# Cached attention with a token mixer: the first keys turned inside the query projection, and a head's closing matmuls placed right behind scores

## The chip, the core and the metric

The kernel runs on one core of a Trainium2 chip. The core has five engines that run in parallel, each with its own queue of instructions that it works off in order: TensorE (PE in the profile), VectorE (DVE), ScalarE (ACT), GpSimd (POOL) and SyncE (SP), which here only issues transfers. They wait for each other through semaphores. Sixteen DMA engines move data between the chip's large memory (HBM) and the core's own (SBUF); matmuls write to a third memory, PSUM, of eight banks. The metric is the time of one execution in microseconds; less is better.

## The reference

Eight sequences, one token each, of width 512. The normalized token is projected to 32 query heads of 128; each group of four query heads shares one of 8 cached key/value heads of 8192 positions. The attention's output is projected back to 512. Beside it runs a mixer whose token axis has length 1, so that it is a sum over 1792 hidden units of a gelu at every one of the 8 x 512 elements. Everything is float32.

```python
xn = layernorm(x)                                # (8, 1, 512)
q = (xn @ wq) as (b, 32 heads, 1, 128)
p = softmax(q . k_cache * 128**-0.5)             # k_cache, v_cache: (8, 8, 8192, 128)
a = (p . v_cache) as (b, 1, 4096) @ wo           # four query heads per cached head
u = gelu(layernorm(xn)[b, d] * w1[f] + b1[f])    # (b, 512, 1792)
return x + a + sum_f u * w2[f] + b2
```

Keys and values are 64 pieces of 4 MB each; all else that is read is small beside them, but for the two projection matrices of 8 MB.

## The kernel before

The work is cut into 64 *pairs* (a cached head h and a sequence b), eight pairs to a head, in the order h, b. One pair takes 4 MB of keys and 4 MB of values. Two buffers hold keys (K, tiles k0 and k1) and two hold values (V, v0 and v1), picked by whether b is even. At the start the value buffers hold the query projection's matrix (`load_wq`, L59). In what follows "key n" and "value n" are those of pair n, counted from the program's start or within a head.

A pair is `slot` (L336). Its instructions are written in one order for all engines, and each engine keeps that order:

- `q_place` (L211) spreads the next pair's query into a weight tile W.
- `qk` (L222) computes the scores of this pair into a PSUM tile (S), 16 matmuls of 512 columns. They need the key *turned*, that is transposed in blocks on VectorE.
- `load(K, ...)` (L65) issues the key after next. Its buffer is the one that `qk` has just read, so it waits for these scores.
- `turn` (L218) transposes the next pair's key, a quarter at a time; the four calls are strewn over the slot. They wait for that key to land.
- `sm_max`, `sm_bias`, `sm_exp`, `sm_place` (L231 to L246) are the softmax: a maximum on VectorE, a small matmul (L236) and two VectorE steps for the bias, the exponential on ScalarE, a matmul (L245) and a transpose on VectorE that put the probabilities in place (PT).
- `pv` (L250) multiplies the pair before's probabilities with its values; `load(V, ...)` behind it issues the next pair's value into the buffer of the pair before, so it waits for these matmuls.
- `o_pick` and `o_place` (L257, L263) gather the result of the pair before into the PSUM tile MH.

Once per head there is more. In the head's first pair (b = 0) stand `o_sums` (L273: the softmax denominators of the last head, four matmuls and a reciprocal) ahead of the exponential, and behind `sm_place` come `o_scale`, `o_project` (L283: the output projection of the last head) and `mx_begin` (L293: a matmul that spreads the mixer's input for this head, and its copy to SBUF by ScalarE). The mixer itself has 14 steps per head (`mx_step`, L300), a gelu on ScalarE and a multiply and an add on GpSimd each, two behind each pair from b = 0 on (three behind each pair in the last head, b = 1 to 4). `mx_end` (L306) sums GpSimd's accumulator ACC into the output with four small matmuls, at the end of a head's last pair (of pair 5 in the last head). `load_wo` (L75) fetches the 1 MB of projection weights for the head, behind pair 2.

The first pair is written ahead of a loop, the loop's body holds pairs 1 to 7 of a head and pair 0 of the next, and the last head's pairs are written out behind it (L382 to L415), with a tail of its own for pairs 6 and 7. Inside the loop the instructions wait by counts within a stage of two pairs; a wait of the loop's first instructions on work ahead of the loop is a wait for the last such work of that engine.

The profile's names: `s` scores, `o` value products, `mh` the tile MH, `misc` the three small PSUM tiles, `pr` and `pt` probabilities before and after placing, `mr`, `sq`, `nb` the softmax's maximum and bias, `macc` the mixer's accumulator, `g` a gelu, `hb` the mixer's input, `om` and `ob` the gathered values.

## Time and profile before

| | us |
|---|---|
| median of 3 runs | 1311.59 (1311.26 to 1312.59) |
| the profiled execution | 1310.17 |
| its span, first to last instruction | 1306.7 |
| DVE busy | 814.9 (62%) |
| PE busy | 788.5 (60%) |
| ACT busy | 289.4 (22%) |
| POOL busy | 252.3 (19%) |
| DMA engines busy, mean over the span | 99% |
| mean granted TensorE clock | 0.764 of full |

The span is what the trace shows; the execution's time has some 3.5 us around it. In the rows below, a view of groups or of a timeline has the start in us, the duration in us, the engine, the line of the kernel, the operation and the tiles (out <- in); a chain has start, duration and what it was. `SPq` is the issue of a transfer, not the transfer itself.

### The profile page before, as it was taken

To read this page: it belongs to the slowest core of one execution; us is meant where nothing else is said; L and a number is where in the kernel's file an instruction comes from. 1 tells how busy PE (TensorE), PEld (TensorE's weight loads), DVE (VectorE), ACT (ScalarE), POOL (GpSimd) and SP (SyncE) were. 2 spreads that over 40 slices of the span, in tenths; PEclk is the share of its full clock that TensorE was granted. 3 is DMA by queue.
4 is the path that set the end of the run, shared out by engine and by line. 5 is a ranking of instruction groups with operands and counts; after the bars stand their busy time and mean duration, and the time that the engine had idled before them with its cause. 6 is when DMAs were issued, how large, how long until landed. Compare 5 with 4: busy or idle time off the path is not lost.

```text
span 1306.7 us, 13701 instructions
## 1 busy us (share of the span) xinstructions
PE 788.5 (60%) x5178; PEld 257.3 (20%) x5178; DVE 814.9 (62%) x860; ACT 289.4 (22%) x365; POOL 252.3 (19%) x226
## 2 busy tenths in 40 slices
PE   3466465755477475665566664575655864757657
PEld 2111112211122121211122111121112211222112
DVE  2664766756657656566656747657566666566574
ACT  0032210313213122132122222022130231202320
POOL 0022120222103121122211221112220221203320
PEclk9787686787768777786876877867767677777779
DMA  9999999999999999999999999999999999999998
GB/s 402 390 381 419 433 433 433 418 417 433 433 433 433 431 433 433 433 433 426 433 433 427 421 436 432 433 426 428 433 433 433 408 433 433 433 433 399 433 423 338
DMA packets 24452, 553.93 MB, mean 424 GB/s; under 512 B 2509, under 2 KB 2541, under 8 KB 6901
## 3 DMA queue, kind: packets, MB, share of 16 engines
q1 hardware_dynamic: 24292, 553.67, 98.9%
q8 instruction: 12, 0.20, 0.1%
q0 software_dynamic: 128, 0.02, 0.0%
q10 hardware_dynamic: 16, 0.02, 0.0%
q14 instruction: 4, 0.02, 0.0%
HBM read 553.69 MB, written 0.02 MB: 424 GB/s over the span
## 4 chain that ended last, share of the span: by engine, by line
DMA 45%; PE 24%; DVE 21%; ACT 5%; issue 1%; DVEq 0%; SPq 0%; POOL 0%; ACTq 0%
DMA k<-in_A_k_cache_dram 43%; DVE k L220 17%; PE s L226 14%; PE misc L245 5%; ACT L241 2%; DMA v<-in_A_v_cache_dram 2%; ACT pr L241 2%; DVE mr L232 1%; PE o L253 1%; PE misc L297 1%; PE misc L287 1%; PE misc L276 1%; DVE nb L238 1%; DVE sq L237 0%; DVE pt L246 0%
## 5 line engine op out<-in xcount | busy, mean ns | idle before, releaser
L220 DVE STREAM_TRANSPOSE k<-k 128x2048 f32<-128x2048 f32 x256 | 581.8, 2293 | 306.3 <-DMA k<-in_A_k_cache_dram 306.0
L226 PE MATMUL s<-k,w 128*32 128x512 f32 x2048 | 314.1, 766 | 18.1 <-DVE k L220 10.9
L253 PE MATMUL o<-v,pt 128*32 128x512 f32 x2048 | 231.9, 592 | 0.9 <-DVE pt L246 0.8
L264 PE MATMUL mh<-sel,ob 128*128 128x4 f32 x126 | 34.7, 346 | 323.9 <-DVE ob L261 323.9
L302 POOL TENSOR_TENSOR g<-g,w2t 128x512 f32<-128x512 f32 x104 | 108.3, 1041 | 627.7 <-ACT g L301 627.7
L241 ACT ACT_TABLE_LOAD x55 | 70.6, 1283 | 604.8 <-DVE nb L238 604.8
L245 PE MATMUL misc<-pr,perm 128*128 128x512 f32 x128 | 128.2, 1104 | 23.4 <-ACT pr L241 21.2
L304 POOL TENSOR_TENSOR macc<-macc,g 128x512 f32<-128x512 f32 x104 | 132.6, 1275 | 9.6
L226 PEld LDWEIGHTS s<-k,w 128*32 128x32 f32 x2048 | 73.4, 139 | 282.3 <-issue 233.2
L301 ACT ACTIVATE g<-hb,b1t,w1t 128x512 f32<-128x512 f32 x112 | 91.0, 813 | 136.5 <-POOL macc L304 126.6
L236 PE MATMUL misc<-nident,mr 128*128 128x128 f32 x128 | 32.9, 341 | 113.3 <-DVE mr L232 113.3
L264 PEld LDWEIGHTS mh<-sel,ob 128*128 128x128 f32 x126 | 29.2, 288 | 337.9 <-DVE ob L261 337.1
L253 PEld LDWEIGHTS o<-v,pt 128*32 128x32 f32 x2048 | 62.0, 110 | 158.3 <-issue 156.0
L241 ACT ACTIVATE pr<-s,nb 128x512 f32<-128x512 f32 x64 | 44.0, 688 | 167.2 <-PE misc L276 147.2
L302 POOL TENSOR_TENSOR macc<-g,w2t 128x512 f32<-128x512 f32 x8 | 8.3, 1041 | 371.1 <-ACT g L301 371.1
L246 DVE STREAM_TRANSPOSE pt<-misc 128x512 f32<-128x512 f32 x64 | 45.8, 716 | 46.3 <-PE misc L245 46.3
L232 DVE TENSOR_REDUCE mr<-s 128x1 f32<-128x512 f32 x64 | 42.3, 661 | 48.2 <-PE s L226 48.1
L301 ACT ACT_TABLE_LOAD x54 | 69.3, 1283 | 1.3
L236 PEld LDWEIGHTS misc<-nident,mr 128*128 128x128 f32 x128 | 20.0, 197 | 169.6 <-DVE mr L232 157.0
L258 DVE TENSOR_TENSOR om<-o,dm 128x512 f32<-128x512 f32 x63 | 42.9, 680 | 0.0
L245 PEld LDWEIGHTS misc<-pr,perm 128*128 128x128 f32 x128 | 30.7, 298 | 30.6 <-ACT pr L241 28.8
L212 DVE TENSOR_TENSOR w<-qt,imask 128x128 f32<-128x128 f32 x64 | 30.9, 483 | 6.9 <-DVE bw L296 4.7
(78 smaller groups left out, 235.4 us busy)
## 6 DMA issues: line engine op xcount, KB each, us to landing
v<-in_A_v_cache_dram SPq DMA_DIRECT2D x63, 4096.0 KB, 27.8
k<-in_A_k_cache_dram SPq DMA_DIRECT2D x62, 4096.0 KB, 21.5
v<-in_A_wq_dram SPq DMA_DIRECT2D x2, 4096.0 KB, 12.6
k<-in_A_k_cache_dram SPq DMA_DIRECT2D x8, 1024.0 KB, 24.5
wo<-in_A_wo_dram SPq DMA_DIRECT2D x7, 1024.0 KB, 26.5
v<-in_A_v_cache_dram SPq DMA_DIRECT2D x1, 2048.0 KB, 13.1
v<-in_A_v_cache_dram SPq DMA_DIRECT2D x1, 1024.0 KB, 14.7
v<-in_A_v_cache_dram SPq DMA_DIRECT2D x2, 512.0 KB, 15.5
```

The lines of the kernel that those rows point to most:

```text
L220: nc.vector.transpose(t, t)
L226: nc.tensor.matmul(S[b % 2][g * Q:(g + 1) * Q, :], W[b % 2][:, j, :], kt[:, g, :, j * Q:(j + 1) * Q], start=(j == 0), stop=(j == NB - 1))
L232: nc.vector.tensor_reduce(MR, S[b % 2], AX.X, ALU.max)
L236: nc.tensor.matmul(m[:, :P], MR.to_broadcast([P, P]), nident, start=True, stop=True)
L241: nc.scalar.activation(PR[b % 2], S[b % 2], AF.Exp, bias=NBIAS, scale=SCALE, accum_out=LR[:, b:b + 1])
L245: nc.tensor.matmul(m, perm, PR[b % 2], start=True, stop=True)
L246: nc.vector.transpose(PT[b % 2], m)
L253: nc.tensor.matmul(O[b % 2][c * Q:(c + 1) * Q, :], PT[b % 2][:, u * Q:(u + 1) * Q], V[b % 2][:, u * NG:(u + 1) * NG, :].rearrange("p t d - ...
L264: nc.tensor.matmul(MH[:, b * REP:(b + 1) * REP], OB[:, :DH], sel, start=True, stop=True)
L301: nc.scalar.activation(G, HB, AF.Gelu_apprx_tanh, bias=b1t[:, j:j + 1], scale=w1t[:, j:j + 1])
L302: nc.gpsimd.tensor_tensor(G if j else ACC, G, w2t[:, j:j + 1].to_broadcast([P, D]), ALU.mult)
L304: nc.gpsimd.tensor_add(ACC, ACC, G)
```

## The change

Six edits, all of order; no arithmetic is added or taken away.

1. `q_project` takes a callback and calls it in each of its halves, ahead of VectorE's copies of the half: the first key's four turns stand there (three in the first half, one in the second) instead of behind the projection.
2. The second value is loaded in the preamble, right behind the first. So pair 0 at the program's start issues no value any more.
3. The head's closing matmuls move. `o_sums` and `mx_end` stand in the next head's pair 0 right behind `qk`, `o_project` and the matmul of `mx_begin` in its pair 1 right behind `qk`. The VectorE and ScalarE steps that read them are split off (`o_recip`, `y_add`, `mx_pick`, `mx_copy`) and stand further back in the same slots. All of them write to free columns of MH now (`sums`, `proj`, `mixed`) instead of the `misc` tiles.
4. The mixer's steps start in a head's pair 1 instead of pair 0. In the last head three stand behind each of the pairs 2 to 5, and `mx_end` follows the scores of pair 6. In the very first head the copy and two steps stand in pair 1 ahead of the exponential.
5. The projection weights are loaded behind pair 3 instead of pair 2.
6. The loop starts one pair later: pairs 0 and 1 stand ahead of it, its body holds pairs 2 to 7 and the next head's 0 and 1.

On SyncE, at the start, with the first value's load as the first row (in the names, v1_87 is the second value buffer, k0_84 the first key buffer; the branches are the loop's entry), before:

```order
L69 DMA v0_86<-in_A_v_cache_dram 128x8192
L69 DMA k0_84<-in_A_k_cache_dram 128x8192
L69 DMA v1_87<-in_A_v_cache_dram 128x8192
L373 COMPARE_AND_BRANCH
L373 UNCONDITIONAL_BRANCH
L441 BRANCH_PREFETCH_HINT
L69 ISA
L69 DMA k1_85<-in_A_k_cache_dram 128x8192
```

and with the change:

```order
L69 DMA v0_86<-in_A_v_cache_dram 128x8192
L69 DMA v1_87<-in_A_v_cache_dram 128x8192
L69 DMA k0_84<-in_A_k_cache_dram 128x8192
L69 DMA k1_85<-in_A_k_cache_dram 128x8192
L69 DMA v0_86<-in_A_v_cache_dram 128x8192
L397 COMPARE_AND_BRANCH
L397 UNCONDITIONAL_BRANCH
L468 BRANCH_PREFETCH_HINT
L69 ISA
L69 DMA k0_84<-in_A_k_cache_dram 128x8192
```

The second value moved ahead of key 2, and two more transfers stand ahead of the loop, whose first is now key 4 instead of key 3.

On TensorE, at a head's end and the next head's start inside the loop, from the last matmul of pair 7 to the branch back (rows of `s` are scores, of `o1` values), before:

```order
L245 MATMUL misc0_174<-pr1_157,perm_123 128x512
L309 MATMUL misc2_176<-macc_165,bw_168 32x128 x4
L226 MATMUL s0_169<-k0_84,w0_152 32x512 x16
L253 MATMUL o1_172<-v1_87,pt1_155 32x512 x16
L236 MATMUL misc1_175<-nident_119,mr_161 128x128
L264 MATMUL mh_173<-sel_121,ob_159 128x4
L276 MATMUL misc0_174<-lr_151,sel_121 128x8 x4
L245 MATMUL misc1_175<-pr0_156,perm_123 128x512
L287 MATMUL misc0_174<-wo_88,ots_149 32x128 x16
L297 MATMUL misc2_176<-hn_189,bm_167 128x512
L373 REGISTER_ALU
L373 COMPARE_AND_BRANCH
```

and with the change, from the same place:

```order
L247 MATMUL misc0_174<-pr1_157,perm_123 128x512
L228 MATMUL s0_169<-k0_84,w0_152 32x512 x16
L279 MATMUL mh_173<-lr_151,sel_121 128x8 x4
L319 MATMUL mh_173<-macc_165,bw_168 32x128 x4
L255 MATMUL o1_172<-v1_87,pt1_155 32x512 x16
L238 MATMUL misc1_175<-nident_119,mr_161 128x128
L266 MATMUL mh_173<-sel_121,ob_159 128x4
L247 MATMUL misc0_174<-pr0_156,perm_123 128x512
L228 MATMUL s1_170<-k1_85,w1_153 32x512 x16
L293 MATMUL mh_173<-wo_88,ots_149 32x128 x16
L306 MATMUL misc2_176<-hn_189,bm_167 128x512
L255 MATMUL o0_171<-v0_86,pt0_154 32x512 x16
```

The sums (lr) and the mixer's end (macc) stand behind the scores of pair 0, the projection (wo) and the mixer's beginning (hn) behind those of pair 1; between the placing of pair 0's probabilities (pr0) and the next scores nothing is left.

On TensorE, in the last head, from the last matmul of pair 5 to the last scores, before:

```order
L245 MATMUL misc0_174<-pr1_157,perm_123 128x512
L309 MATMUL misc2_176<-macc_165,bw_168 32x128 x4
L226 MATMUL s0_169<-k0_84,w0_152 32x512 x16
L236 MATMUL misc1_175<-nident_119,mr_161 128x128
L253 MATMUL o1_172<-v1_87,pt1_155 32x512 x16
L245 MATMUL misc0_174<-pr0_156,perm_123 128x512
L226 MATMUL s1_170<-k1_85,w1_153 32x512 x16
```

and with the change:

```order
L247 MATMUL misc0_174<-pr1_157,perm_123 128x512
L228 MATMUL s0_169<-k0_84,w0_152 32x512 x16
L319 MATMUL mh_173<-macc_165,bw_168 32x128 x4
L238 MATMUL misc1_175<-nident_119,mr_161 128x128
L255 MATMUL o1_172<-v1_87,pt1_155 32x512 x16
L247 MATMUL misc0_174<-pr0_156,perm_123 128x512
L228 MATMUL s1_170<-k1_85,w1_153 32x512 x16
```

The mixer's end moved behind the scores of pair 6, and stands ahead of the bias matmul (L238) and of the values of pair 5.

The core of the diff (the new small functions are the pieces of the old ones that they are split from):

```diff
-    def q_project():
+    def q_project(between):
...
             nc.scalar.copy(qs, mt.rearrange("p (h r b) -> p h r b", h=hw, b=Q)[:, :, :, :B])
+            between(a)
             mq = misc()
...
+    sums = MH[:, 64:64 + REP * B]
+
     def o_sums():
-        m = misc()
         for r in range(REP):
-            nc.tensor.matmul(m[:, r * B:(r + 1) * B], ...)
-        nc.vector.reciprocal(RD, m[:, :REP * B]...)
+            nc.tensor.matmul(sums[:, r * B:(r + 1) * B], ...)
+
+    def o_recip():
+        nc.vector.reciprocal(RD, sums...)
...
+    proj, mixed = MH[:, P:2 * P], MH[:, 2 * P:3 * P]
...
+    def y_add(m):
+        nc.vector.tensor_add(yacc, m, yacc)
...
-    q_project()
+    def first_turns(a):
+        for k in (range(3), range(3, 4))[a]:
+            turn(0, k * quart)
+
+    q_project(first_turns)
     load(V, vc, 0, 0)
+    load(V, vc, 0, 1)
     q_place(0, 0)
...
         load(K, kc, *after(h, b, 2), (NT // 4,) * 4 if last and b == B - 3 else (NT,))
+        if b == 0 and not first:
+            o_sums()
+            mx_end()
+        if b == 1:
+            if not first:
+                o_project(wo_t)
+            mx_begin()
         turn(b + 1, 0)
         sm_max(b)
+        if b == 0 and not first:
+            o_recip()
         turn(b + 1, quart)
-        if not first:
+        if b or not first:
             pv(b - 1)
-        load(V, vc, *after(h, b, 1))
+            load(V, vc, *after(h, b, 1))
...
-        if b == 0 and not first:
-            o_sums()
+        if b < 2 and not first:
+            y_add(proj if b else mixed)
+        if first and b:
+            mx_copy()
+            mx_step(0)
+            mx_step(1)
         sm_exp(b)
         turn(b + 1, 3 * quart)
         sm_place(b)
         if b == 0:
             if not first:
                 o_scale()
-                o_project(wo_t)
-            mx_begin(h)
-        for j in range(3 * b - 1, min(3 * b + 2, NF)) if last else range(2 * b, min(2 * b + 2, NF)):
+            mx_pick(h)
+        if b == 1 and not first:
+            mx_copy()
+        for j in range(3 * b - 4, 3 * b - 1) if last else range(2 * b - 2, 2 * b) if b and not first else ():
             mx_step(j)
-        if b == 2 and not last:
+        if b == 3 and not last:
             load_wo(h)
-        if b == (B - 3 if last else B - 1):
-            mx_end()
-
-    for a in range(4):
-        turn(0, a * quart)
     tc.prologue_barrier()
     slot(0, 0, first=True)
+    slot(0, 1, first=True)
...
     qk(L - 1)
+    mx_end()
     turn(L, 0)
     turn(L, quart)
     sm_max(L - 1)
     sm_bias()
     sm_exp(L - 1)
+    y_add(mixed)
     turn(L, 2 * quart)
```

More of the change, by code (lines that the diff above doesn't have):

```diff
@@ L271, in o_last @@
                              start=(g == 0), stop=(g == NG - 1))
+    sums = MH[:, 64:64 + REP * B]
     def o_sums():
-        m = misc()
         for r in range(REP):
-            nc.tensor.matmul(m[:, r * B:(r + 1) * B], sel[:, r:r + 1].to_broadcast([P, P]), LR, start=True, stop=True)
-        nc.vector.reciprocal(RD, m[:, :REP * B].rearrange("p (r b) -> p r b", r=REP))
+            nc.tensor.matmul(sums[:, r * B:(r + 1) * B], sel[:, r:r + 1].to_broadcast([P, P]), LR, start=True, stop=True)
+    def o_recip():
+        nc.vector.reciprocal(RD, sums.rearrange("p (r b) -> p r b", r=REP))
     def o_scale():
@@ L281, in o_scale, with mx_pick, mx_begin, mx_copy @@
                                 MH[:, :REP * B].rearrange("p (b r) -> p r b", r=REP), RD, ALU.mult)
+    proj, mixed = MH[:, P:2 * P], MH[:, 2 * P:3 * P]
     def o_project(w):
-        m = misc()
         for r in range(REP):
             for j in range(NB):
-                nc.tensor.matmul(m[j * Q:(j + 1) * Q, :D // NB], OTS[:, r, :], w[:, r, quarter[j]],
+                nc.tensor.matmul(proj[j * Q:(j + 1) * Q, :], OTS[:, r, :], w[:, r, quarter[j]],
                                  start=(r == 0), stop=(r == REP - 1))
-        nc.vector.tensor_add(yacc, m[:, :D // NB], yacc)
-    def mx_begin(h):
-        m = MI[2]
+    def y_add(m):
+        nc.vector.tensor_add(yacc, m, yacc)
+    def mx_pick(h):
         nc.vector.tensor_tensor(BM, ident[:B, bass.ds(h, 1)], ident[:B, bass.ds(h, 1)], ALU.mult)
         nc.vector.tensor_tensor(BW, bsel[:, h, :], bsel[:, h, :], ALU.mult)
-        nc.tensor.matmul(m, BM.to_broadcast([B, P]), hn, start=True, stop=True)
-        nc.scalar.copy(HB, m)
+    def mx_begin():
+        nc.tensor.matmul(MI[2], BM.to_broadcast([B, P]), hn, start=True, stop=True)
+    def mx_copy():
+        nc.scalar.copy(HB, MI[2])
     def mx_step(j):
@@ L306, in mx_end @@
     def mx_end():
-        m = MI[2]
         for j in range(NB):
-            nc.tensor.matmul(m[j * Q:(j + 1) * Q, :D // NB], BW, ACC[:, quarter[j]], start=True, stop=True)
-        nc.vector.tensor_add(yacc, m[:, :D // NB], yacc)
+            nc.tensor.matmul(mixed[j * Q:(j + 1) * Q, :], BW, ACC[:, quarter[j]], start=True, stop=True)
     xnT = SQ.rearrange("p (c q) -> p c q", q=Q)
@@ L323, in attn_mixer_kernel @@
     nc.vector.tensor_copy(yacc, m[:, :D // NB])
-    q_project()
+    quart = NT // 4
+    def first_turns(a):
+        for k in (range(3), range(3, 4))[a]:
+            turn(0, k * quart)
+    q_project(first_turns)
     load(V, vc, 0, 0)
+    load(V, vc, 0, 1)
     q_place(0, 0)
-    quart = NT // 4
-    LAST = N_IT - 1
     def after(h, b, n):
@@ L340, in slot @@
         load(K, kc, *after(h, b, 2), (NT // 4,) * 4 if last and b == B - 3 else (NT,))
+        if b == 0 and not first:
[5 more added lines that the diff above has]
+            mx_begin()
         turn(b + 1, 0)
         sm_max(b)
+        if b == 0 and not first:
+            o_recip()
         turn(b + 1, quart)
-        if not first:
+        if b or not first:
             pv(b - 1)
-        load(V, vc, *after(h, b, 1))
+            load(V, vc, *after(h, b, 1))
         turn(b + 1, 2 * quart)
         sm_bias()
-        if not first:
+        if b or not first:
             o_pick(b - 1)
             o_place((b - 1) % B)
-        if b == 0 and not first:
-            o_sums()
+        if b < 2 and not first:
[4 more added lines that the diff above has]
+            mx_step(1)
         sm_exp(b)
@@ L359, in slot @@
                 o_scale()
-                o_project(wo_t)
-            mx_begin(h)
-        for j in range(3 * b - 1, min(3 * b + 2, NF)) if last else range(2 * b, min(2 * b + 2, NF)):
+            mx_pick(h)
+        if b == 1 and not first:
+            mx_copy()
+        for j in range(3 * b - 4, 3 * b - 1) if last else range(2 * b - 2, 2 * b) if b and not first else ():
             mx_step(j)
-        if b == 2 and not last:
+        if b == 3 and not last:
             load_wo(h)
-        if b == (B - 3 if last else B - 1):
-            mx_end()
-    for a in range(4):
-        turn(0, a * quart)
     tc.prologue_barrier()
     slot(0, 0, first=True)
+    slot(0, 1, first=True)
     with tc.For_i(0, HKV - 1, 1, iteration_sync="staggered", head_align_engines=[nc.tensor.engine]) as h:
-        for b in range(1, B):
-            slot(h, b)
-            if b % 2:
+        for b in range(2, B + 2):
+            slot(*after(h, b, 0))
+            if b % 2 == 0:
                 for e in (nc.tensor, nc.vector, nc.scalar, nc.gpsimd):
                     tc.previous_stage_wait(e.engine)
-            else:
+            elif b < B + 1:
                 tc.stage_boundary()
-        slot(h + 1, 0)
     h = HKV - 1
-    for b in range(1, B - 2):
+    for b in range(2, B - 2):
         slot(h, b, last=True)
@@ L410, in attn_mixer_kernel @@
     o_sums()
+    o_recip()
     for u0, u1 in ((8, 12), (12, 14), (14, 16)):
@@ L415, in attn_mixer_kernel @@
     o_project(wo_end)
+    y_add(proj)
     nc.sync.dma_start(out.rearrange("b s (j n) -> j (b s) n", j=NB), yacc[::BS, :])
```

## The prediction

> **What bounds the kernel now.** I read the page's bandwidth row first, since a kernel that streams 554 MB once has a floor there. Each of the 40 slices is 32.67 us.
>
> ```profile
> GB/s 402 390 381 419 433 433 433 418 417 433 433 433 433 431 433 433 433 433 426 433 433 427 421 436 432 433 426 428 433 433 433 408 433 433 433 433 399 433 423 338
> HBM read 553.69 MB, written 0.02 MB: 424 GB/s over the span
> ```
>
> The row has a ceiling, 433, and never holds above it. 553.69 MB at 433 GB/s is 1278.7 us, so 28 us of the 1306.7 us span are stretches in which the transfers ran dry or had not begun. Only those can be won. A split by stretches (columns: stretch, length, granted clock, DMA share, GB/s) says where they lie:
>
> ```profile
> 20.00:110.00 90.00, 0.81 0.94 396
> 110.00:1210.00 1100.00, 0.75 1.00 429
> ```
>
> The first lost (433-396)/433 x 90 = 7.7 us, the second 4/433 x 1100 = 10.2 us (429 is rounded, so 9 to 11.4). Next comes the timeline of the start: the queue's issues, and who was late there (in brackets an engine's idle time and its releaser).
>
> ```profile
> 34.14 0.33 SPq L69 DMA_DIRECT2D v<-in_A_v_cache_dram  x1
> 52.71 0.33 SPq L69 DMA_DIRECT2D k<-in_A_k_cache_dram  x1
> 69.61 0.81 ACT L301 ACTIVATE g<-hb,b1t,w1t 128x512 f32<-128x512 f32 x1 [1.22 <-POOL macc L302]
> 70.57 1.94 PE L226 MATMUL s<-k,w 128*32 128x512 f32 x8 [4.92 <-ACT g L301]
> ```
>
> The chain that ended last has, for the same stretch, the four turns of the first key and key 3's way from issue to landing:
>
> ```profile
> 38.56 8.80 DVE k L220 x4
> 76.48 12.16 DMA k<-in_A_k_cache_dram
> ```
>
> One 4 MB transfer is 4.194/433 = 9.7 us. Issued to a dry queue it took 12.16 us, so issue to landing costs 2.5 us beside its bytes. Key 2, issued at 52.71 behind the first scores, found the queue dry, and so did key 3 at 76.48: with key 2 and value 1 ahead of it, an unbroken queue would have landed key 3 at 52.71 + 2.5 + 3 x 9.7 = 84.3, not at 88.6. That dry spell is 4.3 us, and the one ahead of key 2 is about 3.2 (7.7 less 4.3 and some 0.2 of ordinary scatter). Key 3 was late because the scores that free its buffer started at 70.57, right behind the mixer's second gelu (69.61 + 0.81): the first scores in the loop wait for everything that ScalarE had issued ahead of the loop.
>
> In the middle I followed the chain that ended last through a head's first pair, and its period from head to head.
>
> ```profile
> 368.52 2.31 DVE k L220
> 378.40 1.73 PE misc L276 x8
> 384.09 2.06 PE misc L287 x32
> 386.57 2.07 PE misc L297 x2
> 388.64 5.38 PE s L226 x32
> 394.22 13.01 DMA k<-in_A_k_cache_dram
> 526.10 2.31 DVE k L220
> 683.63 2.31 DVE k L220
> 841.94 2.31 DVE k L220
> 1001.64 2.31 DVE k L220
> ```
>
> Key 1 lands at 368.52; the key after next is issued at 394.22, 25.7 us later. When a key lands, three transfers are still queued, 29.1 us, less 2.5: an issue up to 26.6 us behind the landing costs nothing. Heads 368 to 526 to 683 take 157.5 us each, just the 68.2 MB of a head at 433. The head from 841.94 takes 159.7, so 2.2 are lost. The first pair stands at the edge and falls over it in some heads.
>
> **What each part does.** The yardstick is an ordinary late pair, without the head's extra work:
>
> ```profile
> 1240.52 2.31 DVE k L220
> 1249.75 0.79 ACT pr L241 x2
> 1250.58 2.07 PE misc L245 x2
> 1252.65 5.03 PE s L226 x32
> 1261.19 28.20 DMA v<-in_A_v_cache_dram
> ```
>
> From landing (1240.52) to the end of the scores (1257.68) it takes 17.2 us.
>
> *Middle.* Sums, projection and mixer matmuls leave the place between softmax and the next scores, where 1.73 + 2.06 + 2.07 and the VectorE steps between them make up the 8.5 us by which 25.7 exceeds 17.2. They now follow the scores, behind the key's issue; TensorE has slack there, since it waits for the next key to land. What stays on VectorE in the first pair is the reciprocal and the mixer's addition. The groups by line (last numbers: busy us, mean ns) have both, and the turn of the probabilities that the start will need:
>
> ```profile
> L246 DVE STREAM_TRANSPOSE pt<-misc 128x512 f32<-128x512 f32 x64 | 45.8, 716 | 46.3 <-PE misc L245 46.3
> L277 DVE RECIPROCAL rd<-misc 128x32 f32<-128x32 f32 x8 | 2.9, 358 | 18.6 <-PE misc L276 18.6
> L310 DVE TENSOR_TENSOR yacc<-misc,yacc 128x128 f32<-128x128 f32 x8 | 2.3, 289 | 0.0
> ```
>
> They are 0.36 + 0.29, so 17.9 us against 26.6 allowed. So the first pair's losses go whole. Of the 10.2 us I take 2.7 off for the seven projection-weight loads, which stay (my split between the two is an estimate, up to 3.7 off): 7.5 us won, from 6.5 to 8.5. Next late is nothing: 8.7 us of cover remain. The pair after it gains 4.1 us of matmuls ahead of its value matmuls; on an ordinary pair TensorE idles longer than that, so nothing. Where the pair runs without waiting for a landing it may be 3 us longer, against the same 8.7.
>
> *Start.* The second value goes to the queue right behind the first at 34.14, since both wait only for the query projection to release their buffers, and its 9.7 us fill the first dry spell. Key 2 then lands at 52.71 + 12.2 - 3.2 + 9.7 = 71.4; to keep the queue unbroken it must be issued by 71.4 - 12.2 = 59.2, key 3 by 68.9 and value 2 by 78.6. The first scores ended at about 52.7; without the 8.8 us of turns ahead of them they end near 44, and the second pair's, 5 to 9 us earlier than today and without the hold, near 60. So the three are in time, key 2 even without the early turns. The mixer steps now stand ahead of the second pair's softmax, where ScalarE waits for a landing anyway, so the 4.9 us hold is gone. What is late next is key 4. When key 2 lands, only two transfers are behind it, not three: key 4 may be issued 19.4 - 2.5 = 16.9 us later. It needs the 17.2 of an ordinary pair, and since its scores are the loop's first they wait for VectorE's last step ahead of the loop too, the 0.7 us turn of the probabilities. That is 1.0 us dry. Entering the loop was never seen bare; I bound it between 0 and the 4.9 us for which TensorE stood there, and take 0.8, near the low end, because that hold has a named releaser. With 1.8 us dry, 4.3 + 3.2 - 1.8 = 5.7 us are won, from 1.6 to 7.5.
>
> *End.* This one costs. The last head's mixer now has three steps in each of pairs 2 to 5 rather than 1 to 4, and its matmuls stand behind the scores of pair 6, ahead of the softmax's bias matmul and of the values of pair 5.
>
> ```profile
> 1250.34 0.19 ACT L241 ACTIVATION_READ_ACCUMULATOR pr<-s,nb 128x1 f32 x1
> 1257.16 1.28 POOL L304 TENSOR_TENSOR macc<-macc,g 128x512 f32<-128x512 f32 x1
> 1260.49 1.28 POOL L304 TENSOR_TENSOR macc<-macc,g 128x512 f32<-128x512 f32 x1
> 1269.84 0.19 ACT L241 ACTIVATION_READ_ACCUMULATOR pr<-s,nb 128x1 f32 x1
> 1272.09 0.66 PE L309 MATMUL misc<-macc,bw 128*32 128x128 f32 x8
> 1272.51 5.37 PE L226 MATMUL s<-k,w 128*32 128x512 f32 x32
> 1278.71 0.49 PE L236 MATMUL misc<-nident,mr 128*128 128x128 f32 x2 [0.82 <-DVE mr L232]
> 1279.13 3.64 PE L253 MATMUL o<-v,pt 128*32 128x512 f32 x32
> 1284.38 3.64 PE L226 MATMUL s<-k,w 128*32 128x512 f32 x32 [0.56 <-DVE k L220]
> 1289.43 3.64 PE L253 MATMUL o<-v,pt 128*32 128x512 f32 x32
> ```
>
> Three steps end 1261.77 - 1250.53 = 11.2 us behind the softmax. In pair 5 that softmax ends at 1270.03, so GpSimd's sum is ready at 1281.3. The scores of pair 6 end at 1277.5 (they start 0.4 sooner, without the mixer matmuls ahead). TensorE stands 3.8 us; then come the mixer matmuls, 0.7, the bias matmul, 0.5, and the values of pair 5 at 1282.5 instead of 1279.13: 3.4 later. Behind them stand the last scores (1284.38) and the values of pair 6 (1289.43), which start today as their value lands, so the whole shift reaches the end. Value 7 is issued behind the values of pair 5, at 1286.2; with value 6 landing at 1289.4 it is in time until 1289.4 - 2.5 = 1286.9, so the transfers just stay unbroken. The values behind the stand may run at a lower clock: scores after idle took 5.37 against 3.64. I bound that between 0 and 1.7 and take 0.6, since the mixer and bias matmuls take the first 1.2 us of a warm-up. End: 4.0 us lost, from 3.4 to 5.1.
>
> The Trainium skill (TensorE: Matmul & The Clock Gate, Part 1: The HAM clock gate) has the array fall to half clock after an idle window of about 3.4 us. By that rule the values run slow for most of their length and the end costs nearer 5.1 than 4.0, and the change would bring 8.1 us rather than 9.2. The 5.37 us scores agree with it.
>
> *Sum.* 7.5 + 5.7 - 4.0 = 9.2 us. The profiled execution, 1310.17 us with its 1306.7 us span, becomes about 1301.0; against the median of 1311.59 that is 1302.4.
>
> **The rivals.** *Entering the loop stalls* (0.14). Key 4's scores would start late by up to the 4.9 us hold, and here the queue is thin, so each microsecond counts: 4.1 more than my 0.8, net 5.1 us, 1306.5. For it: TensorE stood idle for 4.92 us there. Against: the releaser named is ScalarE. The Trainium skill (Runtime: NRT & Kernel Launch, Instruction fetch mechanics) says a taken branch to a page not yet held "forces a DMA fetch of the target page before execution can continue"; it gives no time for it, and no row of before shows such a fetch at the entry.
>
> *The end is hidden* (0.09). If the sum on GpSimd is ready as the scores end, or TensorE passes the mixer matmuls by, the last term is 0: 13.2 us, 1298.4. Against: three steps per pair at 11.2 us are fixed, and nothing stands between the scores and these matmuls.
>
> *The middle's losses are not the first pair's* (0.06). If they come from the transfers themselves, they stay: 5.7 - 4.0 = 1.7 us, 1309.9, within 0.2%. Against: the quiet heads at 157.5.
>
> *Slower* (0.04). In every head TensorE now stops at the mixer matmuls until GpSimd is done. Two steps take 11.2 - 3.3 = 7.9 us behind the softmax; TensorE gets there 2.07 + 5.03 + 1.73 = 8.8 us behind it, so it should not stop. If it stopped for over the 8.7 us of cover, each further microsecond would cost seven; from 10.4 us on the change is slower by over 0.2% (2.6 us, about what a measurement of this kernel can tell from no change). At 11 us the time is 1311.59 - 9.2 + 7 x 2.3 = 1318.5. Only a GpSimd chain more than twice as long as traced does that.
>
> **How the numbers follow.** My forecast has 0.67. The terms' own bounds, taken as independent, reach about 2.1 us down and 4.4 up, 1300.3 to 1306.8, of which the upper end is the stalled entry. The range goes on below, half way to the hidden end, and stops above just short of the full stall: 1299.4 to 1306.2. Faster takes the forecast, the entry and the end: 0.90. Within 0.2% takes the middle's rival, 0.06. Slower 0.04.
>
> **What would show it.** Right: no slice below 425 GB/s from the fourth to the last but one; second value issued by 35 us; key 4's issue near 90 us with a dry spell of 1 to 3 us; first pair 17 to 19 us from landing to issue in every head; TensorE idle some 4 us ahead of the last head's mixer matmuls with GpSimd named. Wrong: dry spells left at the heads, key 4's issue behind 93 us, or no idle at the mixer matmuls.

## The result, and the profile after

The changed kernel takes 1302.33 us, the median of 4 runs (1300.80 to 1302.57). The kernel before, run beside it, took 1312.09 us. The ratio is 0.9923, with a 95% interval from 0.9905 to 0.9940: the change is faster, by 0.8%. The profiled execution took 1302.48 us with a span of 1298.7 us; before it was 1310.17 and 1306.7.

The bandwidth row of the page, over 40 slices of 32.5 us:

```profile
GB/s 403 434 377 435 431 434 432 430 426 441 435 435 428 430 436 435 435 428 431 435 436 434 429 430 435 436 434 430 430 434 436 434 433 428 433 436 434 431 427 268
```

From the fourth slice to the last but one nothing is below 426; the dips to 399 and 408 of before are gone. The third slice is as low as before, and the last, 268, is lower than the 338 of before. The same two stretches as in the prediction (length, granted clock, DMA share, GB/s):

```profile
20.00:110.00 90.00, 0.79 0.97 415
110.00:1210.00 1100.00, 0.76 1.00 433
```

The middle now runs at the ceiling, 433 instead of 429. The start rose from 396 to 415, so (433-415)/433 x 90 = 3.7 us are still lost there, of 7.7.

To split the span into start, middle and end I use two instructions that both kernels have: the first turn of head 1's key 1 and that of the last head's key 6. Each starts as its key lands. From the timeline of VectorE, before:

```profile
209.36 2.31 DVE L220 STREAM_TRANSPOSE k<-k 128x2048 f32<-128x2048 f32 x1 [5.96 <-DMA k<-in_A_k_cache_dram]
1260.02 2.31 DVE L220 STREAM_TRANSPOSE k<-k 128x2048 f32<-128x2048 f32 x1 [6.10 <-DMA k<-in_A_k_cache_dram]
```

and after:

```profile
205.56 2.31 DVE L222 STREAM_TRANSPOSE k<-k 128x2048 f32<-128x2048 f32 x1 [5.94 <-DMA k<-in_A_k_cache_dram]
1247.16 2.31 DVE L222 STREAM_TRANSPOSE k<-k 128x2048 f32<-128x2048 f32 x1 [6.00 <-DMA k<-in_A_k_cache_dram]
```

The start is the time of the first of the two, the middle lies between them, the end is the rest of the span:

| | start | middle | end | span |
|---|---|---|---|---|
| before | 209.4 | 1050.7 | 46.7 | 1306.7 |
| after | 205.6 | 1041.6 | 51.5 | 1298.7 |
| won | 3.8 | 9.1 | -4.9 | 8.0 |
| predicted | 5.7 | 7.5 | -4.0 | 9.2 |

All three signs are as predicted; two of the sizes were off by nearly 2 us, in opposite directions. The rows behind each follow.

*Start.* The timeline of the issues, of key 2's landing, and of what follows it up to key 4's issue (in brackets the idle time before and its releaser):

```profile
35.27 0.81 SPq L69 DMA_DIRECT2D v<-in_A_v_cache_dram  x2
43.45 18.34 SPq L69 DMA_DIRECT2D k<-in_A_k_cache_dram  x2
66.07 0.33 SPq L69 DMA_DIRECT2D v<-in_A_v_cache_dram  x1
72.89 2.31 DVE L222 STREAM_TRANSPOSE k<-k 128x2048 f32<-128x2048 f32 x1 [15.82 <-DMA k<-in_A_k_cache_dram]
83.05 2.05 PE L247 MATMUL misc<-pr,perm 128*128 128x512 f32 x2 [0.27 <-ACT pr L243]
85.97 5.81 PE L228 MATMUL s<-k,w 128*32 128x512 f32 x32 [0.88 <-DVE pt L248]
92.10 0.35 SPq L69 DMA_DIRECT2D k<-in_A_k_cache_dram  x1
```

Both values are issued by 36, key 2 at 43.45, key 3 near 61.5 (the second issue of the row at 43.45, which ends at 61.79) and value 2 at 66.07, all in time. Key 2 lands at 72.89 and key 4 is issued 19.2 us later. The first scores in the loop wait 0.88 us, for the turn of the probabilities. The queue is dry once, between 90 and 100 us:

```profile
90.00:100.00 10.00, 6.21 (x53) 2.07 (x46) 7.84 (x9) 2.30 (x4) 0.00 (x0) 0.98 0.75 295
```

(433-295)/433 x 10 = 3.2 us are lost there, where 1.8 were expected.

*Middle.* The timeline of one head's first pair, the head that starts near 510:

```profile
518.68 1.06 PE L279 MATMUL mh<-lr,sel 128*128 128x8 f32 x8
519.67 0.42 PE L319 MATMUL mh<-macc,bw 128*32 128x128 f32 x8
520.45 2.31 DVE L222 STREAM_TRANSPOSE k<-k 128x2048 f32<-128x2048 f32 x1 [5.88 <-DMA k<-in_A_k_cache_dram]
539.26 0.33 SPq L69 DMA_DIRECT2D k<-in_A_k_cache_dram  x1
```

The sums and the mixer's end run ahead of the landing and wait for nobody. From landing to issue it takes 18.8 us. The same pair before:

```profile
526.10 2.31 DVE L220 STREAM_TRANSPOSE k<-k 128x2048 f32<-128x2048 f32 x1 [5.90 <-DMA k<-in_A_k_cache_dram]
551.52 0.33 SPq L69 DMA_DIRECT2D k<-in_A_k_cache_dram  x1
```

That was 25.4 us. Over the seven first pairs it is 17.3 to 18.8 us now and was 25.4 to 29.2 before.

*End.* The timeline of the tail, from GpSimd's last sum to the values of pair 6:

```profile
1259.23 4.57 PE L228 MATMUL s<-k,w 128*32 128x512 f32 x32
1267.13 1.26 POOL L315 TENSOR_TENSOR macc<-macc,g 128x512 f32<-128x512 f32 x1
1268.44 0.65 PE L319 MATMUL mh<-macc,bw 128*32 128x128 f32 x8 [4.64 <-POOL macc L315]
1269.75 6.13 PE L255 MATMUL o<-v,pt 128*32 128x512 f32 x32
1281.74 3.64 PE L255 MATMUL o<-v,pt 128*32 128x512 f32 x32
```

TensorE stands 4.64 us for GpSimd ahead of the mixer's end. The values behind it take 6.13 us instead of 3.64. Nothing after them waits for a transfer any more: the values of pair 6 are late for TensorE alone. A split of the same stretch shows why they are slow (the last three columns are granted clock, DMA share and GB/s):

```profile
1264.00:1268.00 4.00, 0.00 (x0) 0.00 (x0) 1.55 (x2) 0.81 (x1) 3.00 (x3) 1.00 1.16 498
1268.00:1270.00 2.00, 1.56 (x14) 0.91 (x18) 0.14 (x1) 0.00 (x0) 0.39 (x1) 0.50 0.83 360
1270.00:1276.00 6.00, 6.00 (x33) 1.29 (x26) 5.05 (x5) 2.06 (x3) 0.00 (x0) 0.60 0.94 377
```

In the 2 us behind the stand the granted clock is 0.50, in the next 6 it is 0.60.

### The profile page after: what moved, and what is told of

It is laid out like the page before. It is cut to its first block, busy times and chain, and to the rows that moved or that the text cites. A ratio compares the mean times of both kernels' runs of the same rounds, so it can differ in the third digit from the quotient of the medians.

```text
span 1298.7 us, 13708 instructions
## 1 busy us (share of the span) xinstructions
PE 780.6 (60%) x5178; PEld 250.2 (19%) x5178; DVE 809.2 (62%) x860; ACT 289.8 (22%) x366; POOL 251.8 (19%) x226
## 4 chain that ended last, share of the span: by engine, by line
DMA 52%; DVE 21%; PE 18%; ACT 4%; issue 1%; POOL 1%; SPq 0%; ACTq 0%; DVEq 0%
DMA k<-in_A_k_cache_dram 52%; DVE k L222 17%; PE s L228 12%; PE misc L247 4%; ACT L243 2%; ACT pr L243 1%; DVE mr L234 1%; PE o L255 1%; DVE nb L240 1%; DVE sq L239 0%; PE mh L266 0%; DVE om L260 0%; POOL macc L315 0%; POOL g L313 0%; DVE ob L262 0%
## 5 line engine op out<-in xcount | busy, mean ns | idle before, releaser
L228 PE MATMUL s<-k,w 128*32 128x512 f32 x2048 | 318.4, 774 | 11.5 <-DVE k L222 8.4
L255 PE MATMUL o<-v,pt 128*32 128x512 f32 x2048 | 234.8, 598 | 0.8 <-DVE pt L248 0.8
L238 PE MATMUL misc<-nident,mr 128*128 128x128 f32 x128 | 34.0, 350 | 110.7 <-DVE mr L234 110.7
L238 PEld LDWEIGHTS misc<-nident,mr 128*128 128x128 f32 x128 | 20.8, 204 | 166.6 <-DVE mr L234 160.4
(77 smaller groups left out, 204.6 us busy)
```

The source lines that it names most:

```text
L228: nc.tensor.matmul(S[b % 2][g * Q:(g + 1) * Q, :], W[b % 2][:, j, :], kt[:, g, :, j * Q:(j + 1) * Q], start=(j == 0), stop=(j == NB - 1))
L238: nc.tensor.matmul(m[:, :P], MR.to_broadcast([P, P]), nident, start=True, stop=True)
L255: nc.tensor.matmul(O[b % 2][c * Q:(c + 1) * Q, :], PT[b % 2][:, u * Q:(u + 1) * Q], V[b % 2][:, u * NG:(u + 1) * NG, :].rearrange("p t d - ...
```

## The experiments

Each kernel is the changed kernel with one edit or two, and each has start, middle and end measured as above. In the six kernels whose start was not edited (after, mixer's end later, closing matmuls back, wait filled, only the sums moved, weights earlier) it lies between 204.6 and 205.6, so a start is good to about 1 us. The times come from several chips; each ratio is against the kernel before on the same one, so small differences between two kernels are read from start, middle and end.

| | median us | ratio to before, 95% | start | middle | end |
|---|---|---|---|---|---|
| after | 1302.33 | 0.9923 (0.9905 to 0.9940) | 205.6 | 1041.6 | 51.5 |
| mixer's end later | 1297.65 | 0.9877 (0.9858 to 0.9897) | 205.3 | 1041.7 | 46.5 |
| turns late | 1301.16 | 0.9903 (0.9886 to 0.9919) | 204.5 | 1041.6 | 51.6 |
| second value late | 1297.28 | 0.9878 (0.9858 to 0.9898) | 201.1 | 1042.7 | 49.4 |
| closing matmuls back | 1308.92 | 0.9963 (0.9951 to 0.9976) | 205.4 | 1049.9 | 49.6 |
| wait filled | 1300.54 | 0.9898 (0.9877 to 0.9918) | 204.6 | 1041.6 | 49.4 |
| only the sums moved | 1302.76 | 0.9916 (0.9897 to 0.9936) | 205.0 | 1042.4 | 52.2 |
| value and mixer's end late | 1294.31 | 0.9852 (0.9832 to 0.9872) | 201.6 | 1042.7 | 46.8 |
| turns and value late | 1300.51 | 0.9903 (0.9883 to 0.9922) | 204.9 | 1041.6 | 50.2 |
| warm scores, first try | 1306.84 | 0.9950 (0.9932 to 0.9968) | 210.9 | 1041.5 | 50.2 |
| warm scores | 1300.38 | 0.9909 (0.9893 to 0.9925) | 203.3 | 1042.2 | 50.0 |
| weights earlier | 1301.68 | 0.9903 (0.9888 to 0.9919) | 205.1 | 1041.6 | 55.5 |

### The middle: put the closing matmuls back

```diff
         if b == 0 and not first:
-            o_sums()
             mx_end()
-        if b == 1:
-            if not first:
-                o_project(wo_t)
-            mx_begin()
...
-        if b < 2 and not first:
-            y_add(proj if b else mixed)
+        if b == 0 and not first:
+            y_add(mixed)
+            o_sums()
+            o_recip()
...
             if not first:
                 o_scale()
+                o_project(wo_t)
+                y_add(proj)
             mx_pick(h)
+            mx_begin()
```

(The `o_recip` further up goes, and the mixer's end stays behind the scores.)

> The changed kernel with the sums ahead of the first pair's exponential and the projection and mixer-begin matmuls ahead of the second pair's scores, as before; the mixer's end and its steps stay where the change put them. Theory (the first pair's way from landing to issue sets the middle's dry spells): they come back, 7 to 9 us lost, 1309.5 to 1311, and the stretch from 110 to 1210 us falls from 433 to about 429 GB/s. Rival (the middle's dry spells came from the mixer's steps, which now start a pair later, or from the loop's branch, which now lies a pair later): no change, 1302.3.

The timeline of the same head's first pair, from landing to issue:

```profile
521.90 2.31 DVE L222 STREAM_TRANSPOSE k<-k 128x2048 f32<-128x2048 f32 x1 [5.88 <-DMA k<-in_A_k_cache_dram]
548.98 0.33 SPq L69 DMA_DIRECT2D k<-in_A_k_cache_dram  x1
```

That is 27.1 us here, and 25.8 to 27.3 over the seven heads. The middle takes 1049.9 us: 8.3 of the 9.1 us are back, at 1308.92 us in all. The median rose by 6.6 us only, since the tail's values ran at full clock here (end 49.6). The middle's gain comes from these matmuls.

The edge over which the pair falls is not sharp. In this kernel first pairs of 25.8 and 26.3 us made key 3 land no later, another of 25.9 made it land 2.0 us later, and the longest, 27.3, 2.4 us later. Before the change one of 26.6 lost nothing, one of 26.2 lost 2.2 and the longest, 29.2, lost 2.7. What else decides, no run shows.

### The middle: how much has to move?

In this kernel only the sums and the mixer's end stay behind the first pair's scores; projection and mixer's beginning go back between the two pairs.

```diff
         if b == 0 and not first:
             o_sums()
             mx_end()
-        if b == 1:
-            if not first:
-                o_project(wo_t)
-            mx_begin()
...
             if not first:
                 o_scale()
+                o_project(wo_t)
+                y_add(proj)
             mx_pick(h)
+            mx_begin()
```

> The changed kernel with only the sums and the mixer's end behind the first pair's scores; the projection and the mixer's beginning go back between the first pair's softmax and the second pair's scores. Theory (a landing-to-issue time counts only beyond the 26.6 us that the queue covers, so what matters is not how much was moved but whether the pair gets under that bound): without the sums, 1.73 us of matmuls and the reciprocal, the second pair needs some 23 us, so nothing is lost: 1302 to 1303 and 433 GB/s between 110 and 1210 us. Rival (each microsecond moved counts in proportion): two thirds of the 8 us of the middle come back, about 1307, and some 430 GB/s.

The same pair in this kernel's timeline:

```profile
520.06 2.31 DVE L222 STREAM_TRANSPOSE k<-k 128x2048 f32<-128x2048 f32 x1 [5.88 <-DMA k<-in_A_k_cache_dram]
544.85 0.33 SPq L69 DMA_DIRECT2D k<-in_A_k_cache_dram  x1
```

24.8 us instead of 18.8, the longest of the seven heads (23.3 to 24.8), and the middle still takes 1042.4 us, 0.8 more than with everything moved. Three other kernels, with everything moved, have a middle of 1042.2 to 1042.7, so these 0.8 us need not come from the pair. Six microseconds less slack cost almost nothing; the next 2.3 (to the 27.1 above) cost 7.5 over the run. What counts is whether the pair stays within the queue's cover, not how much was moved.

### The middle: is it the weights' place?

The forecast had set 2.7 us aside for the loads of the projection weights. This kernel loads them behind pair 2 again.

```diff
-        if b == 3 and not last:
+        if b == 2 and not last:
             load_wo(h)
```

> The changed kernel with the projection weights of each head loaded behind pair 2 again, as before the change, instead of behind pair 3. The measure is the stretch from the turn of head 1's key 1 to that of the last head's key 6: 1050.7 us before, 1041.6 with the change, 1049.9 with the closing matmuls put back. Theory (the 1 us by which the change won more in the middle than moving the matmuls explains comes from this place of the load; the forecast took the load's cost as staying): 1042.5 to 1043.5, so the time 1 to 2 us up, 1303.3 to 1304.3. Rival (the first pair's slack absorbs the load wherever it stands): 1041.6 to 1041.9 and 1302.3.

The rows of the two turns, 205.12 and 1246.72:

```profile
205.12 2.31 DVE L222 STREAM_TRANSPOSE k<-k 128x2048 f32<-128x2048 f32 x1 [5.96 <-DMA k<-in_A_k_cache_dram]
1246.72 2.31 DVE L222 STREAM_TRANSPOSE k<-k 128x2048 f32<-128x2048 f32 x1 [5.98 <-DMA k<-in_A_k_cache_dram]
```

1041.60 us between them, the same as after to the hundredth. My theory falls: in this kernel the place of the load is worth nothing. (The profiled execution was the longest of the five, 1306.0 us; in the table its last matmuls, slow as well, make the end 55.5. The median is 1301.68.)

### The end: does the stand reach the end?

The mixer's end goes one place further back, behind the placing of pair 6's probabilities.

```diff
     qk(L - 1)
-    mx_end()
...
     sm_exp(L - 1)
-    y_add(mixed)
...
     sm_place(L - 1)
+    mx_end()
     qk(L)
     o_pick(L - 2)
+    y_add(mixed)
```

> The changed kernel, but the last head's mixer matmuls stand behind the placing of pair 6's probabilities instead of behind its scores, and their addition behind the gathering of pair 5. Theory (TensorE stands 4.6 us there and then runs the values of pair 5 at a low clock, 6.13 us against 3.64; 4.9 us of it reach the end): 4.9 us off, 1297.4 us; the values of pair 5 take about 3.7 us and no idle time of TensorE names GpSimd in the tail. Rival (the tail is set by the last transfers, so the wait is hidden): no change, 1302.3. Second rival (only the clock counts, the stand is covered): 1.5 us off, 1300.8.

The tail of this kernel:

```profile
1259.05 5.09 PE L228 MATMUL s<-k,w 128*32 128x512 f32 x32
1265.84 3.64 PE L255 MATMUL o<-v,pt 128*32 128x512 f32 x32
1270.47 0.43 PE L319 MATMUL mh<-macc,bw 128*32 128x128 f32 x8
1271.10 3.64 PE L228 MATMUL s<-k,w 128*32 128x512 f32 x32 [0.20 <-DVE k L222]
1276.22 3.64 PE L255 MATMUL o<-v,pt 128*32 128x512 f32 x32 [0.17 <-DMA v<-in_A_v_cache_dram]
```

No stand, full clock, and the values of pair 6 wait for their transfer again. The end is 46.5, that of before, and the time 1297.65 us. All of the end's 4.9 us come from that one place in the order.

### The end: the stand or the clock behind it?

Four matmuls whose result nobody reads fill a part of the stand.

```diff
     qk(L - 1)
+    for _ in range(4):
+        nc.tensor.matmul(MI[2], perm, PR[1], start=True, stop=True)
     mx_end()
```

> The changed kernel with four added 512-column matmuls on TensorE between the last-but-one scores (pair 6) and the mixer's end; nothing reads their result. They fill about half of the 4.6 us for which TensorE stands there, and delay nothing, since GpSimd's sum is late anyway. Theory (the values of pair 5 took 6.13 us instead of 3.64 because TensorE had stood 4.6 us): they take 3.64, the stand's end stays where GpSimd puts it, and of the 2.5 us about 1.5 reach the end: 1300.8. Rival A (the values are slow for another reason, as the copies around them or the transfer): 6.1 us again and 1302.3. Rival B (added matmuls push the mixer's end back): slower than 1303.

```profile
1262.55 3.70 PE L412 MATMUL misc<-pr,perm 128*128 128x512 f32 x8
1267.55 0.42 PE L319 MATMUL mh<-macc,bw 128*32 128x128 f32 x8 [1.30 <-POOL macc L315]
1268.32 3.64 PE L255 MATMUL o<-v,pt 128*32 128x512 f32 x32
```

In this kernel's tail the idle time ahead of the mixer's end is 1.30 us, GpSimd is still the releaser, and the values take 3.64. The end falls from 51.5 to 49.4. So of the 4.9 us, 2.7 are the stand (49.4 against 46.7) and 2.2 the slow clock behind it; matmuls that nobody reads win these 2.2 back.

### The start: the turns, the second value, and both

Three kernels undo the two edits of the start, singly and together. The first puts the turns back behind the projection.

```diff
-    q_project(first_turns)
+    q_project(lambda a: None)
...
+    for a in range(4):
+        turn(0, a * quart)
     tc.prologue_barrier()
```

> The changed kernel with the first key's four turns behind the query projection, as before; the second value stays early. Theory (key 2 may be issued until about 59 and key 3 until about 69; without the early turns they come near 52 and 69): no change beyond 1 us, 1302 to 1303, with the dry spell ahead of key 4 as it is, 2.7 to 3.5 us. Rival (the early turns bring the gain at the start): 3 us or more lost, 1305 or above, with a second dry spell ahead of key 2 or 3.

Start 204.5 against 205.6, little more than what the start is good to: with the second value early, the early turns win nothing. Key 2 lands at about the same time, since the second value's transfer stands ahead of it in either case.

The second kernel issues the second value inside pair 0, as before the change, and keeps the early turns.

```diff
     load(V, vc, 0, 0)
-    load(V, vc, 0, 1)
...
         if b or not first:
             pv(b - 1)
-            load(V, vc, *after(h, b, 1))
+        load(V, vc, *after(h, b, 1))
```

> The changed kernel with the second value issued in the first pair, behind key 2, as before; the early turns stay. Theory (early turns alone put key 2 in the queue at 43.5, ahead of the first value's end, so the early value fills nothing, and by its place ahead of key 2 it leaves only two transfers behind key 2's landing, which makes the dry spell ahead of key 4): that dry spell goes, 2.7 to 3.5 us off, 1298.8 to 1299.6, and the stretch from 20 to 110 us runs at 430 GB/s or above. Rival, the prediction's view (the early value fills the first dry spell): 3.2 us lost, 1305.5.

Key 2's issue and landing and key 4's issue in its timeline:

```profile
42.87 0.33 SPq L69 DMA_DIRECT2D k<-in_A_k_cache_dram  x1
63.06 2.31 DVE L222 STREAM_TRANSPOSE k<-k 128x2048 f32<-128x2048 f32 x1 [6.47 <-DMA k<-in_A_k_cache_dram]
81.54 0.36 SPq L69 DMA_DIRECT2D k<-in_A_k_cache_dram  x1
```

Key 2 lands 9.8 us sooner, one whole transfer, with value 1 behind it. Key 4 again needs 18.5 us from there, but now it has three transfers for cover, and there is no dry spell (430 GB/s from 20 to 110 us): start 201.1, 4.4 us better than with the change. The prediction had given the early second value the credit for filling the first dry spell; the early turns fill it by themselves, and the early value only takes a transfer from key 4's cover. The time fell by more than the theory's 3.5 us because the tail's values ran at full clock here (end 49.4), while the middle took 1.1 us more:

```profile
1265.14 0.43 PE L319 MATMUL mh<-macc,bw 128*32 128x128 f32 x8 [3.54 <-POOL macc L315]
1265.91 3.64 PE L255 MATMUL o<-v,pt 128*32 128x512 f32 x32
```

The third kernel has both edits undone.

> The changed kernel with both edits of the start undone: the first key's turns behind the query projection again, and the second value issued inside the first pair. Theory (the early turns are what fills the first dry spell once the second value isn't issued early): key 2 is issued near 52 us, the first dry spell of about 3.2 us is back, the one ahead of key 4 stays away: about 1300.5 to 1302, against 1297.3 with the early turns. Rival (the early turns are worth nothing, as they were with the second value early): 1297 to 1298 and 430 GB/s between 20 and 110 us.

Start 204.9 and 1300.51 us: with the second value late, the early turns are worth 3.8 us. So the four starts are 205.6 (both early), 204.5 (value early), 201.1 (turns early), 204.9 (neither), against 209.4 before the change. The last step, 4.5 us, is what the other edits bring at the start, the moved mixer steps among them. Its scores of pair 1 and the issue of key 3 behind them show where:

```profile
62.71 4.48 PE L228 MATMUL s<-k,w 128*32 128x512 f32 x32
67.26 0.33 SPq L69 DMA_DIRECT2D k<-in_A_k_cache_dram  x1
```

Before the change these scores started at 70.57, behind the mixer's matmul and its second gelu, and key 3 was issued at 76.48. So the hold is gone with neither of the two edits, and the two together win nothing at the start (205.6 against 204.9): what the change won there comes from the other edits (the mixer's matmul and steps further back, the loop entered a pair later), which were not taken apart.

This kernel's tail shows a stand hardly longer than the one above, with slow values:

```profile
1267.76 0.42 PE L319 MATMUL mh<-macc,bw 128*32 128x128 f32 x8 [3.62 <-POOL macc L315]
1268.53 5.34 PE L255 MATMUL o<-v,pt 128*32 128x512 f32 x32
```

### The start: the late landing or slow scores?

Key 4's dry spell was 3.2 us and not 1.8. Four idle matmuls are to warm TensorE ahead of the scores that free key 4's buffer.

```diff
         sm_bias()
+        if first and b:
+            for _ in range(4):
+                nc.tensor.matmul(MI[2], perm, PR[0], start=True, stop=True)
```

> The changed kernel with four added 512-column matmuls on TensorE in the program's second pair, behind the bias matmul, where it stands from 76.6 to 82.2 us; nothing reads their result. They end before the next matmul is due. Theory (of the dry spell of 3.5 us ahead of key 4, a good part is that the scores of pair 2 run on a TensorE that has idled: 5.81 us instead of 3.64, and the placing matmul ahead of them 2.05 instead of about 1): scores of pair 2 near 3.7, key 4 issued 2 to 3 us earlier, 0.5 to 1.5 us dry, 1302.3 - 2.5 = 1300 (1299 to 1300.5). Rival A (the dry spell is the late landing of key 2 alone): 3.5 us dry again, 1302.3. Rival B (the scores are slow for another reason than the clock, such as code fetched at the loop's entry): 5.8 us again, 1302.3.

```profile
76.05 5.30 PE L373 MATMUL misc<-pr,perm 128*128 128x512 f32 x8
81.39 0.59 ACT L309 COPY hb<-misc 128x512 f32<-128x512 f32 x1 [27.91 <-PE misc L373]
88.31 2.05 PE L247 MATMUL misc<-pr,perm 128*128 128x512 f32 x2 [6.11 <-ACT pr L243]
97.81 0.35 SPq L69 DMA_DIRECT2D k<-in_A_k_cache_dram  x1
```

This run does not answer the question. The added matmuls write to the tile that holds the mixer's input, ahead of its copy to SBUF, so the first head's mixer part of the output is changed, and ScalarE's copy (81.39) and with it the softmax wait for them. The placing starts 5.3 us later than with the change, and the start moves by 5.4 (210.9). So a delay at this place reaches the transfers in full, as the prediction's rival of a stalled loop entry had assumed; the entry itself did not stall. The second try writes to the tile that the placing uses next.

```diff
-                nc.tensor.matmul(MI[2], perm, PR[0], start=True, stop=True)
+                nc.tensor.matmul(MI[0], perm, PR[0], start=True, stop=True)
```

> The run before once more, with the four added matmuls written to the tile that the placing matmul uses next, which nobody reads until then; so ScalarE's copy of the mixer's input no longer waits for them. Theory as there: the placing matmul of pair 1 starts at 83 as in the changed kernel and takes about 1.1 us, the scores of pair 2 near 3.7, key 4 is issued near 89, the dry spell is 0.5 to 1.5 us, and the time 1299 to 1300.5. Rival A (the late landing of key 2 alone makes the dry spell): 3.5 us and 1302.3. Rival B (the scores are slow for another reason than the clock): 5.8 us and 1302.3.

```profile
76.00 4.90 PE L373 MATMUL misc<-pr,perm 128*128 128x512 f32 x8
82.63 1.10 PE L247 MATMUL misc<-pr,perm 128*128 128x512 f32 x2 [0.47 <-ACT pr L243]
84.61 3.64 PE L228 MATMUL s<-k,w 128*32 128x512 f32 x32 [0.88 <-DVE pt L248]
88.56 0.35 SPq L69 DMA_DIRECT2D k<-in_A_k_cache_dram  x1
```

Placing 1.10 instead of 2.05, scores 3.64 instead of 5.81, key 4 issued 3.5 us sooner (0.4 of it because key 2 landed sooner). The start falls to 203.3, the time to 1300.38 us; with 426 GB/s from 20 to 110 us some 1.5 us are still lost there. Both rivals fall: the spell is not the landing alone, and the scores at the loop's entry were slow through the clock.

### Both repairs together

> The changed kernel with the second value issued inside the first pair as before the change, and the last head's mixer end one place later (behind the placing of pair 6's probabilities). Theory (the start's dry spell ahead of key 4 and the end's stand are two separate losses): the start gains about 3.5 us as with the second value alone, the end 4.9 as with the later mixer end alone: 1302.3 - 4.9 - 3.5 = 1294, TensorE nowhere standing for GpSimd at the end and 430 GB/s between 20 and 110 us. Rival (the end is bound by the last value's landing, or by something that the other edit hid): no more than the better one alone, 1297.

1294.31 us, ratio 0.9852 (0.9832 to 0.9872): start 201.6, end 46.8. The two losses are separate and add up: the start gains 4.0 us and the end 4.7, and the middle takes 1.1 us more, as with the second value late alone. By the medians this version is 8.0 us faster than the change, and it beats both kernels.

## Why the prediction was right

The way was as forecast, but the time, 1302.33 us against 1302.4, came out closer than its terms, and that is luck. The middle won 1.6 us more than forecast, the start 1.9 less, and the end lost 0.9 more. So the profiled execution, forecast at 1301.0, took 1302.48: 7.7 us won, not 9.2. What hides this is that the median of before runs 1.4 us above its profiled execution; median against median, on one chip, 9.8 us were won.

- **Middle: right in its mechanism, undersized.** 9.1 us against 7.5 (6.5 to 8.5). The first pairs fell to 17.3 to 18.8 us, inside the 17 to 19 foretold, and putting the matmuls back took back 8.3. The bound of 26.6 us was too sharp: the 25.7 us pair of the prediction lost nothing, and in the kernel with the matmuls put back one of 25.9 lost 2.0. The step that failed is the 2.7 us taken off for the weight loads, which were to stay. In the changed kernel they cost nothing beyond their bytes, at either place: a head takes 157.4 to 157.5 us, just its bytes at 433 GB/s. That they had cost something before only because the first pair had just thinned the queue is my reading; no run shows it by itself.
- **Start: right in its sign, oversized.** 3.8 us against 5.7. Of the missing 1.9, the dry spell explains 1.4; the rest is within what the start is good to. The hold at the mixer's second gelu went as foretold, and the remaining spell did move to key 4. The failed step is "With 1.8 us dry". Key 4 needed 19.2 us from key 2's landing where 18.7 were reckoned, and had 19.2 - 3.2 = 16.0 us of cover where 16.9 were. So half a microsecond came on the one side, 0.9 on the other. The 4.3 us set down for the hold came out at 4.5; what failed in net is the 3.2 for the first dry spell, since the same 3.2 us came back ahead of key 4. Of the time needed, 3.1 us is TensorE's clock, as the warm scores show (5.81 + 2.05 against 3.64 + 1.10); the ordinary pair from which I took 17.2 has a part of that too.
- **The second value: wrong.** That "its 9.7 us fill the first dry spell" is true, but the early turns would have filled it alone, and with both edits one undoes the other. I noted that the early turns were not needed for key 2 and did not draw the other half: that then the early value isn't needed either, and takes the third transfer from key 4's cover.
- **End: right in its mechanism, undersized.** 4.9 us against 4.0. The stand was 4.64 us with GpSimd named; its share of the end was 2.7 where 3.4 were reckoned, and the clock's 2.2 where I took 0.6. (Some 0.5 of the difference is only where it is counted: the mixer and bias matmuls ran slow as well, 0.65 and 0.80 us against 0.42 and 0.49 with the wait filled.) The failed step is that "the mixer and bias matmuls take the first 1.2 us of a warm-up": the granted clock stayed low for most of the 6 us behind. The Trainium skill's rule (TensorE: Matmul & The Clock Gate, Part 1: The HAM clock gate), which I had set beside it, would have made the end 5.1 and the change 8.1 us; the traces give 4.9 and 8.0. The trace agrees with the rule and not with my term: the values did run slow for most of their length. That the sums agree so well is luck again, since the stand was reckoned too long, the clock's share too short, and the middle and the start off in opposite directions.
- **The rivals.** The loop's entry did not stall: 0.88 us idle with VectorE named, and full clock right behind it once TensorE was warm. The Trainium skill's fetch at a taken branch (Runtime: NRT & Kernel Launch, Instruction fetch mechanics) shows in no run here. The end was not hidden, the middle's losses were the first pair's, and inside the loop TensorE does not stop at the mixer matmuls in five of seven heads (as in the row at 519.67) and for 0.64 and 0.30 us in the other two, far below what the rival needed.

## What to carry to other kernels

When a stream of transfers bounds a kernel, ask of each landing how many transfers are still queued behind it, and compare that cover with the time from the landing to the next issue: work that fits inside the cover is free wherever it stands, and work beyond it costs. At the start a delay of 5.3 us cost 5.4; at the heads the edge was blurred by a microsecond or so. A prefetch moved forward also moves what is behind it: the early second value put key 2 back by one transfer, which cost 4.4 us at the start. Where an in-order engine must wait for another late in a program, put the waiting instruction behind all the work that is ready, and count the slower clock after the stand as well as the stand.

## What the runs showed of the hardware beyond that

- **The clock behind a stand has a narrow edge here.** Stands of 3.54 and 3.56 us ahead of the mixer's end left the values at 3.64 us; one of 3.62 us made them 5.34. Longer ones, 4.22 to 4.94 us, gave 4.48 to 6.13, and not in order of their length. That is one run each, so where the edge lies is known no better. What sets the amount can be read from finer splits of these tails. The granted clock there is either 0.50 or 1.00, and it stays at 0.50 for about 3.41 us in three kernels (turns and value late, both warm scores) and for about 6.83, twice as long, in four (after, turns late, only the sums moved, weights earlier). It fell to 0.50 between 3.9 and 5.2 us after TensorE had stopped, in two kernels only behind the stand. The values lose half of the part of this stretch that falls on them: after the change it ended at 1274.82, 5.07 us into the values, which took 2.5 us longer. The Trainium skill (TensorE: Matmul & The Clock Gate, Part 1: The HAM clock gate) gives the gate a free-running window of about 3.4 us. The lengths of these stretches agree with it, one window or two; what decides whether a stand of 3.6 us brings one, no run here shows.
- **Queued transfers cover less time than their bytes say.** Issued to a dry queue, a transfer took 12.16 us, 2.5 more than its bytes (12.17 for key 4 after the change). The cover of key 4 was 16.0 us for two transfers of 9.7, so by the estimate of its dry spell 3.4 us are missing there. For three transfers that would make 29.1 - 3.4 = 25.7 us, an estimate; the first pairs of the heads begin to lose near there.
